# Windowed attention and a Mish layer: GpSimd keeps only the sums and maxima over partitions, and VectorE joins and splits the weights

## The chip, the cores and the metric

The kernel runs on one core of one Trainium2 chip. A core has five engines, each with its own queue of instructions that it works through in order, and they wait for each other through semaphores. TensorE (PE in the profile) multiplies matrices; the loading of its stationary operand is listed apart as PEld. VectorE is DVE, ScalarE is ACT, GpSimd is POOL, and SyncE (SP) only issues transfers here. ScalarE issues transfers too: all loads of the weights. The metric is the time of one execution on the device in microseconds (us).

## The reference

The program is an attention stage followed by a two-matrix layer. There are 8 batches of 8 heads; each head has 512 local positions and 32 global ones of width 64. A local query sees the 32 global keys and the local keys at a distance of at most 32. A global query sees everything.

```python
s_g = scale * np.matmul(q_g, k_all.transpose(0, 1, 3, 2))
out_g = np.matmul(sm(s_g), v_all)
s_ll = np.where(mask, s_ll, -1000000000.0)      # |i - j| <= 32
a_l = sm(np.concatenate([s_lg, s_ll], axis=-1))
out_l = np.matmul(a_l, np.concatenate([v_g, v_l], axis=2))
...
h = x @ w_in                                    # 4352 tokens, 512 -> 2048
g = h * np.tanh(np.log1p(np.exp(h)))            # for h <= 20
return (g @ w_out).astype(np.float32)           # 2048 -> 512
```

The inputs of the attention stage are 32-bit floats. The two weight matrices `w_in` and `w_out` arrive as 64-bit floats, and the kernel itself turns them into 32-bit ones from their two 32-bit words.

## The kernel before, in words

**Precision.** Matrix products run in 16-bit halves: an operand is scaled by a power of two, its high part is rounded to 16 bits, and its low part is what the rounding left. A product is then three matmuls (high by high, high by low, low by high). For the power of two, the kernel needs a maximum over all partitions (for the values `v`, one per batch) or a sum of squares over them (for each weight matrix). GpSimd makes both with `partition_all_reduce`: L504 for the maxima, L428 for the sums.

**The weights.** They come in 32 pieces of 512 KB, 16 for each matrix, loaded by ScalarE's queue (`w_load`, L379 and L383). For each piece, `w_bits` and `w_sum` build the 32-bit word. VectorE takes mantissa and exponent bits from the high word (L396), ScalarE turns the low word into a rounded integer `wr` (L398), VectorE puts in sign and top of the exponent (L405), and GpSimd adds `wr` as an integer (L407), so that a carry is right. Then TensorE adds the piece's squares into `ws` (`w_stat`, L417). After 16 pieces VectorE takes the diagonal of `ws` (L424), GpSimd sums it (L428), and a short chain gives the scale (L429 to L434). `w_split` then makes the halves, eight slots of 128x1024 for each matrix. For the first five slots of the first matrix, ScalarE or VectorE makes the high part directly and VectorE the low part (L452). For the other eleven, two ScalarE or VectorE steps make a scaled copy and the high part, and GpSimd subtracts them for the low part (L457).

**The attention.** 128 units (batch, pair of heads, 128 queries) run in a software pipeline: scores on TensorE (L613 for the first five head pairs in plain 32 bits, L620 after), a row minimum on VectorE (L626), exponentials on ScalarE (L635), high and low part of the result (L319, L654), a transposing transfer (L479), and the product with `v` (L671). Before any of it can be finished for the first batch, `v` has to be split with the scale that L504 to L512 make: L524 and L526 for the global rows, L319 and L573 for the local ones.

**The layer.** 17 blocks of 256 tokens in eight steps each: matmuls of the first matrix (`m1_mm`, L800), the Mish function on ScalarE (L843), high and low part (L321, L856), matmuls of the second matrix (`m2_mm`, L868). The first step of the first block stands at attention unit 17, and one step goes with each unit from there.

**What sets the order.** The program doesn't issue instructions as it meets them. `Plan.add` records each piece of work with an engine (or a choice of two), a cost in nanoseconds and what it reads and writes; `Plan.order` is a list scheduler that assigns start times from these costs, and the instructions are issued to the engines in that order. Weights have due times of their own (`CONV1`, `RATE1`, `FIRST1` and so on). A cost changed in `add` thus moves other instructions, on all engines. On the chip each engine keeps to its list, whatever the real durations are.

Of the kernel before, what the change touches and what calls it, by code (L numbers as in the profile page):

```python
# [226 lines left out]
def attn_mish_kernel(ctx: ExitStack, tc: tile.TileContext, qt, kt, qt0, kt0, vm, vg, qg, w1, w2, consts_in, out, w64):  # L227
# [13 lines left out]
    iww = const.tile([128, 1], F32, name="iww")  # L241
    W = const.tile([128, 18, 1024], F32, name="W")
# [5 lines left out]
    def rings(pool, *table):  # L248
        for tag, bufs, shape, dt in table:
# [5 lines left out]
          ("wr", 2, [128, 512], I32),  # L255
# [36 lines left out]
    def act(cols, acc=0):  # L292
        return 94 + 0.832 * cols + acc * 93
# [98 lines left out]
    def w_bits(k):  # L392
        if not w64:
# [4 lines left out]
        pl.add(ACT, act(512), lambda: A.activation(out=X["wr", k], in_=words(k).bitcast(U32)[:, :, 0], func=AF.Copy,  # L398
                                                   scale=2.0 ** -29), r=[rawkey(k)], new=[("wr", ("wr", k))])

    def w_sum(k):
        if not w64:
            return
        f, key = lambda: wf(k).bitcast(I32), wkey(*HV[k])
        pl.add(DVE, 680, lambda: V.scalar_tensor_tensor(f(), words(k)[:, :, 1], -0x40000000, f(), ALU.bitwise_and, ALU.bitwise_or),  # L405
               r=[rawkey(k)], w=[key])
        pl.add(POOL, 1400, lambda: G.tensor_tensor(f(), f(), X["wr", k], ALU.add), r=[("wr", k)], w=[key])  # L407
# [13 lines left out]
    def w_norm(w):  # L421
# [6 lines left out]
        pl.add(POOL, 4500, lambda: G.partition_all_reduce(X[p], X[m], 128, RED.add), r=[m], new=[("p2", p)])  # L428
# [11 lines left out]
    ON_POOL = 3  # L440

    parted = set()

    def w_split(j):
# [5 lines left out]
        if j < 8 - ON_POOL:  # L450
            pl.add([(ACT, act(1024)), (DVE, dve2(1024))], 0, lambda e: scaled(e, wh(j, 0), f, c), r=[k, ["sw", w]], w=[wslot(j)])
            pl.add(DVE, dve(1024), lambda: V.scalar_tensor_tensor(wh(j, 1), f, c, wh(j, 0), ALU.mult, ALU.subtract),  # L452
                   r=[k, ["sw", w], hi], w=[lo])
        else:
            pl.add([(ACT, act(1024)), (DVE, dve2(1024))], 0, lambda e: scaled(e, f, f, c), r=[["sw", w]], w=[k])
            pl.add([(ACT, act(1024)), (DVE, dve2(1024))], 0, lambda e: copy(e, wh(j, 0), f), r=[k], w=[wslot(j)])
            pl.add(POOL, 2230, lambda: G.tensor_tensor(wh(j, 1), f, wh(j, 0), ALU.subtract), r=[k, hi], w=[lo])  # L457

# [42 lines left out]
    def b_scale(b):  # L501

        m, p, sv = ("vmx", b), ("p2", b), ("sv", b)
        pl.add(POOL, 4500, lambda: G.partition_all_reduce(X[p], X[m][:, 5:6], 128, RED.max), r=[m], new=[("p2", p)])  # L504
# [565 lines left out]
    V.memset(pmax, 0.0)  # L1070
    for x in ORDER.split():
# [90 lines left out]
```

## Time and profile before

| what | value |
|---|---|
| median of 3 runs | 1037.8 us (1035.43 to 1037.85) |
| profiled execution, span | 1037.7 us, 20569 instructions |
| PE busy | 926.5 us (89%) |
| DVE busy | 664.3 us (64%) |
| ACT busy | 686.4 us (66%) |
| POOL busy | 85.2 us (8%), 62 instructions |

The profiled execution's time is its span, 1037.7 us, which is 0.1 us from the median of the runs. A page of the profile lists busy time by engine, the span in 40 slices of about 26 us with the busy share of each engine in tenths, and groups of instructions by line. A group's row names the line, the engine, the operation, output and input, a count, and then busy us, the mean ns of one, and the idle time of the engine just before, with the instruction that ended it. A row of the timeline is: start in us, duration in us, engine, line, operation, output<-input, and in square brackets the idle time just before and what ended it. "issue" there means that nothing which the profile records was waited for. GpSimd's loading of code is such a thing: it has no row as work.

### The profile page before, as it was taken

Reading aid. Unit: us, or ns where it says so; the run is one execution under the profiler, and the core shown is the slowest. Engines: PE = TensorE matmul, PEld = TensorE weight load, DVE = VectorE, ACT = ScalarE, POOL = GpSimd, SP = SyncE. Lnnn points to the kernel's source line nnn. Section 1 sums busy time; section 2 is a strip of 40 time slices with the busy share of each in tenths; the row PEclk is TensorE's granted clock in tenths of the full one; section 3 lists DMA queues with packets and bytes.
Section 4 is the critical chain, followed back from the end, with each engine's and each line's share of the span. In section 5 each row is a group of like instructions: output and inputs, shape, how many; then the busy total and the mean of one; then the engine's idle time right before and its main releaser. Section 6 shows DMA issues by size and latency. Waiting matters only on the chain.

```text
span 1037.7 us, 20569 instructions
## 1 busy us (share of the span) xinstructions
PE 926.5 (89%) x7906; PEld 665.6 (64%) x7906; DVE 664.3 (64%) x1697; ACT 686.4 (66%) x1327; POOL 85.2 (8%) x62
## 2 busy tenths in 40 slices
PE   3166558899999999999999999999999999999996
PEld 1044336567777777777777777677777777666663
DVE  4397977778766776677667766776676765422221
ACT  1257648677687888878887888788978887311110
POOL 3333531500000000000000000000000000000000
PEclk9997558999999999999999999999999999999998
DMA  9686792377866666667666665656675634100000
GB/s 358 232 199 138 158 197 83 88 162 161 187 145 140 145 144 151 136 144 143 138 150 143 136 140 136 148 121 140 145 157 120 141 75 79 28 21 21 1 21 21
DMA packets 231802, 134.65 MB, mean 130 GB/s; under 512 B 197528, under 2 KB 209048, under 8 KB 230680
## 3 DMA queue, kind: packets, MB, share of 16 engines
q1 hardware_dynamic: 225048, 116.56, 51.2%
q10 hardware_dynamic: 6656, 16.78, 5.0%
q8 instruction: 62, 1.02, 0.4%
q14 instruction: 36, 0.29, 0.1%
HBM read 63.55 MB, written 8.91 MB: 70 GB/s over the span
## 4 chain that ended last, share of the span: by engine, by line
PE 61%; DVE 11%; DMA 8%; ACT 6%; SPq 2%; issue 2%; POOL 0%; ACTq 0%; DVEq 0%; POOLq 0%
PE o L868 26%; PE h L800 25%; PE s L620 4%; DMA vraw<-in_vm 3%; PE U L671 3%; PE g L709 2%; DMA gpt<-gph 2%; SPq L308 2%; ACT L843 1%; PE gu L757 1%; DVE ph L654 1%; DVE P L626 1%; DVE vmx L493 1%; DMA W<-in_w 1%; ACT e L843 1%
## 5 line engine op out<-in xcount | busy, mean ns | idle before, releaser
L800 PE MATMUL h<-xh,W 128*128 128x256 f16 x2048 | 380.5, 275 | 11.0 <-ACT e L843 11.0
L868 PE MATMUL o<-W,G 128*128 128x512 f16 x1632 | 388.3, 379 | 0.2 <-POOL W L457 0.2
L800 PEld LDWEIGHTS <-W 128*128 128x128 f16 x3264 | 310.9, 98 | 74.2 <-issue 12.0
L800 PE MATMUL h<-xl,W 128*128 128x256 f16 x1024 | 281.3, 275 | 0.0
L868 PEld LDWEIGHTS <-G 128*128 128x128 f16 x1632 | 157.5, 98 | 145.9 <-issue 0.5
L843 ACT ACTIVATE e<-h,c 128x512 f32<-128x512 f32 (+1 forms) x137 | 92.8, 683 | 125.2 <-PE h L800 124.4
L626 DVE CUSTOM_DVE_ANT_0 P<-s,consts 128x192 f32<-128x192 f32 (+1 forms) x256 | 90.4, 366 | 86.8 <-PE s L620 84.5
L635 ACT ACTIVATE P<-P,nm 128x192 f32<-128x192 f32 (+1 forms) x256 | 118.0, 461 | 34.8 <-DVE nm L626 29.9
L321 DVE TENSOR_SCALAR G<-e,c 128x512 f16<-128x512 f32 x129 | 62.0, 480 | 120.2 <-ACT e L843 119.9
L654 DVE SCALAR_TENSOR_TENSOR ph<-P,ph 128x384 f16<-128x384 f32 (+1 forms) x128 | 80.6, 633 | 65.4 <-ACT ph L319 65.1
L856 DVE SCALAR_TENSOR_TENSOR G<-e,c,G 128x512 f16<-128x512 f32 (+1 forms) x137 | 103.8, 758 | 4.2 <-ACT G L319 1.0
L843 ACT ACT_TABLE_LOAD x78 | 100.1, 1283 | 1.4
L635 ACT ACT_TABLE_LOAD x75 | 96.2, 1283 | 1.3
L671 PEld LDWEIGHTS <-pt 96*128 96x128 f16 (+1 forms) x1536 | 59.3, 101 | 28.0 <-DMA pt<-ph 20.4
L319 ACT ACTIVATE ph<-P 128x384 f16<-128x384 f32 (+1 forms) x128 | 69.3, 546 | 12.1 <-DMA pt<-ph 9.1
L671 PE MATMUL U<-va,pt 128*128 128x64 f16 (+1 forms) x768 | 59.5, 200 | 16.4 <-DMA pt<-ph 15.1
L620 PE MATMUL s<-ks,qs 128*128 128x192 f32 (+1 forms) x216 | 70.7, 351 | 1.2 <-ACT gP L730 1.1
L417 PE MATMUL ws<-W 128*128 128x128 bf16 x128 | 18.9, 299 | 57.4 <-POOL W L407 57.2
L671 PE MATMUL U<-vc,pt 96*128 96x64 f16 x768 | 58.9, 198 | 0.0
L407 POOL TENSOR_TENSOR W<-W,wr 128x512 int32<-128x512 int32 x32 | 48.3, 1520 | 80.6 <-DVE W L405 17.7
L417 PEld LDWEIGHTS <-W 128*128 128x128 bf16 x128 | 10.9, 127 | 67.5 <-POOL W L407 65.1
L620 PE MATMUL s<-kl,qs 128*128 128x192 f32 (+1 forms) x216 | 54.2, 274 | 0.0
(102 smaller groups left out, 1049.8 us busy)
## 6 DMA issues: line engine op xcount, KB each, us to landing
kraw<-in_kt SPq DMA_DIRECT2D x27, 640.0 KB, 4.9
qraw<-in_qt SPq DMA_DIRECT2D x27, 512.0 KB, 3.8
W<-in_w ACTq DMA_DIRECT2D x19, 512.0 KB, 4.9
out<-ob SPq DMA_DIRECT2D x34, 256.0 KB, 2.6
vraw<-in_vm SPq DMA_DIRECT2D x8, 1024.0 KB, 5.9
wraw<-in_w ACTq DMA_DIRECT2D x13, 512.0 KB, 9.3
vc<-vf SPq DMA_DIRECT2D x32, 128.0 KB, 2.3
va<-vf SPq DMA_DIRECT2D x32, 96.0 KB, 2.3
```

The source lines that it names most:

```text
L319: A.activation(out=dst, in_=src, func=AF.Copy, scale=c)
L321: V.tensor_scalar(dst, src, c, None, ALU.mult)
L407: pl.add(POOL, 1400, lambda: G.tensor_tensor(f(), f(), X["wr", k], ALU.add), r=[("wr", k)], w=[key])
L620: T.matmul(X[s][:, :w], X[qs][:, h, t * 128:(t + 1) * 128], X[k][:, h, c0:c0 + w], start=(i == 0), stop=(i == 1))
L626: pl.add(DVE, 69 + 1.04 * w, lambda: V.tensor_tensor_reduce(out=X[P][:, h, :w], in0=X[s][:, :w], in1=mask[:, m0:m0 + w], scale=-SCALE, sca ...
L635: pl.add(ACT, 160 + 0.832 * w + 93, lambda: A.activation(out=X[P][:, h, :w], in_=X[P][:, h, :w], func=AF.Exp, bias=X[nm], scale=-1.0, accu ...
L654: pl.add(DVE, dve(n), lambda: V.scalar_tensor_tensor(p_part(X[ph], t, 1), p_src(X[P], t), PSC, p_part(X[ph], t, 0), ALU.mult, ALU.subtract ...
L671: T.matmul(X[u][:, t, h, :], X[pt][:k, p * 4 + h * 2 + c, :], X[vx][:k, t, vl, h * 64:(h + 1) * 64], start=(n == 0), stop=(n == 5))
L800: T.matmul(X[h][:, f * TB:(f + 1) * TB], wh(i, wl)[:, off:off + 128], X[x][:, d, o:o + TB], start=(n == 0), stop=(n == 11))
L843: chain(blk, i, ACT, 571, lambda a, z: A.activation(out=X[e][:, a:z], in_=hv(blk, i)[:, a:z], func=AF.Mish, bias=0.0, scale=X[c][:, 0:1]), ...
L856: chain(blk, i, DVE, 602, lambda a, z: V.scalar_tensor_tensor(gp(1, blk, i)[:, a:z], X[e][:, a:z], X["c", blk][:, 2:3], gp(0, blk, i)[:, a ...
L868: T.matmul(X[o], gp(g, blk, i)[:, f, t * 128:(t + 1) * 128], wh(8 + i, wl)[:, f * 512:(f + 1) * 512], start=(i == 0 and n == 0), stop=(i = ...
```

## The change

GpSimd's integer additions (L407) and subtractions (L457) go. VectorE puts in the low word itself, shifted by 29 bits and without rounding, in one more pass for each piece; ScalarE's conversion (L398) and its buffer `wr` go with the addition. All sixteen slots are split in the short way, with VectorE making every low part. GpSimd's list begins, behind its five memsets, with a maximum over a vector of zeros whose result nobody reads. The planner's cost for the sums and maxima goes from 4500 to 900, that of the dummy is 14000.

```diff
-          ("wr", 2, [128, 512], I32),
...
     def w_bits(k):
...
-        pl.add(ACT, act(512), lambda: A.activation(out=X["wr", k], in_=words(k).bitcast(U32)[:, :, 0], func=AF.Copy,
-                                                   scale=2.0 ** -29), r=[rawkey(k)], new=[("wr", ("wr", k))])
...
     def w_sum(k):
...
-        pl.add(DVE, 680, lambda: V.scalar_tensor_tensor(f(), words(k)[:, :, 1], -0x40000000, f(), ALU.bitwise_and, ALU.bitwise_or),
+        pl.add(DVE, 610, lambda: V.scalar_tensor_tensor(f(), words(k)[:, :, 1], -0x40000000, f(), ALU.bitwise_and, ALU.bitwise_or),
                r=[rawkey(k)], w=[key])
-        pl.add(POOL, 1400, lambda: G.tensor_tensor(f(), f(), X["wr", k], ALU.add), r=[("wr", k)], w=[key])
+        pl.add(DVE, 610, lambda: V.scalar_tensor_tensor(f(), words(k)[:, :, 0], 29, f(), ALU.logical_shift_right, ALU.bitwise_or),
+               r=[rawkey(k)], w=[key])
...
-        pl.add(POOL, 4500, lambda: G.partition_all_reduce(X[p], X[m], 128, RED.add), r=[m], new=[("p2", p)])
+        pl.add(POOL, 900, lambda: G.partition_all_reduce(X[p], X[m], 128, RED.add), r=[m], new=[("p2", p)])
...
-    ON_POOL = 3
...
-        if j < 8 - ON_POOL:
-            pl.add([(ACT, act(1024)), (DVE, dve2(1024))], 0, lambda e: scaled(e, wh(j, 0), f, c), r=[k, ["sw", w]], w=[wslot(j)])
-            pl.add(DVE, dve(1024), lambda: V.scalar_tensor_tensor(wh(j, 1), f, c, wh(j, 0), ALU.mult, ALU.subtract),
-                   r=[k, ["sw", w], hi], w=[lo])
-        else:
-            pl.add([(ACT, act(1024)), (DVE, dve2(1024))], 0, lambda e: scaled(e, f, f, c), r=[["sw", w]], w=[k])
-            pl.add([(ACT, act(1024)), (DVE, dve2(1024))], 0, lambda e: copy(e, wh(j, 0), f), r=[k], w=[wslot(j)])
-            pl.add(POOL, 2230, lambda: G.tensor_tensor(wh(j, 1), f, wh(j, 0), ALU.subtract), r=[k, hi], w=[lo])
+        pl.add([(ACT, act(1024)), (DVE, dve2(1024))], 0, lambda e: scaled(e, wh(j, 0), f, c), r=[k, ["sw", w]], w=[wslot(j)])
+        pl.add(DVE, dve(1024), lambda: V.scalar_tensor_tensor(wh(j, 1), f, c, wh(j, 0), ALU.mult, ALU.subtract),
+               r=[k, ["sw", w], hi], w=[lo])
...
-        pl.add(POOL, 4500, lambda: G.partition_all_reduce(X[p], X[m][:, 5:6], 128, RED.max), r=[m], new=[("p2", p)])
+        pl.add(POOL, 900, lambda: G.partition_all_reduce(X[p], X[m][:, 5:6], 128, RED.max), r=[m], new=[("p2", p)])
...
     V.memset(pmax, 0.0)
+    pl.add(POOL, 14000, lambda: G.partition_all_reduce(warm, pmax, 128, RED.max))
```

Three places of the instruction order are shown here, before and after. A row gives the line in the kernel concerned (lines below the edits move up by 8 or 9), the operation, the output, and behind the arrow the inputs.

The first is GpSimd's list from its last memset on. A row "ISA" with no operands is the loading of a set of operations into the engine; `vmx` holds the maxima of `v`, `wm` the diagonal of `ws`. Before:

```order
L281 MEMSET gph_80 64x1280
L407 ISA
L407 TENSOR_TENSOR W<-W,wr_115 128x512
L407 TENSOR_TENSOR W<-W,wr_134 128x512
L407 TENSOR_TENSOR W<-W,wr_152 128x512
L504 ISA
L504 ISA p_0_197<-vmx_154 128x1
L407 ISA
L407 TENSOR_TENSOR W<-W,wr_170 128x512
```

After:

```order
L281 MEMSET gph_81 64x1280
L1062 ISA
L1062 ISA warm<-pmax 128x1
L495 ISA p_0_181<-vmx_141 128x1
L427 ISA wp_399<-wm_391 128x1
L427 ISA wp_1474<-wm_1469 128x1
L495 ISA p_1_1492<-vmx_1152 128x1
```

Before, additions and maxima take turns, and each turn has a loading row: eight in the whole list. After, there is one such row, ahead of the dummy, and the rest of the list is ten sums and maxima.

The second is ScalarE's list around the split of the first batch's global rows of `v` (`vgf`), the first thing there that needs the scale from the first maximum. `wraw` and `W` behind "DMA" are loads of weight pieces. Before:

```order
L383 DMA wraw_195<-in_w 128x1024
L398 ACTIVATE wr_204<-W 128x512
L635 ACTIVATE P_0_1_138,sums_0_163<-P_0_1_138,nm_0_1_0_139 128x224
L319 ACTIVATE ph_72<-P_0_0_120 128x4x96
L383 DMA wraw_209<-in_w 128x1024
L383 DMA wraw_212<-in_w 128x1024
L398 ACTIVATE wr_225<-W 128x512
L524 ACTIVATE vgf_232<-vgraw_100,sv_217 128x128
```

After:

```order
L626 ACTIVATE P_0_0_117,sums_0_139<-P_0_0_117,nm_0_0_0_118 128x192
L379 DMA W<-in_w 128x2x512
L379 DMA wraw_150<-in_w 128x2x512
L379 DMA wraw_152<-in_w 128x2x512
L379 DMA wraw_158<-in_w 128x2x512
L383 DMA wraw_164<-in_w 128x1024
L383 DMA wraw_168<-in_w 128x1024
L383 DMA wraw_170<-in_w 128x1024
L515 ACTIVATE vgf_192<-vgraw_102,sv_184 128x128
```

In both, `vgf` stands behind the load of the nineteenth piece. The conversions `wr`, which waited for GpSimd's additions to free their two buffers, are gone from between.

The third is VectorE's list at the same place, from the first step on the maximum `p` on. Before:

```order
L508 TENSOR_SCALAR p_0_197<-p_0_197 128x1
L325 TENSOR_SCALAR p_0_197<-p_0_197 128x1
L328 TENSOR_SCALAR sv_217<-p_0_197 128x1
L329 RECIPROCAL sv_217<-sv_217 128x1
L511 TENSOR_SCALAR sv_217<-sv_217 128x1
L512 TENSOR_TENSOR pmax<-pmax,p_0_197 128x1
L396 TENSOR_SCALAR W<-W 128x512 x2
L526 SCALAR_TENSOR_TENSOR vgf_232<-vgraw_100,sv_217,vgf_232 128x128
L405 SCALAR_TENSOR_TENSOR W<-W 128x512 x2
L573 SCALAR_TENSOR_TENSOR vf_0_234<-vraw_96,sv_217,vf_0_234 128x4x128
```

After:

```order
L499 TENSOR_SCALAR p_0_181<-p_0_181 128x1
L325 TENSOR_SCALAR p_0_181<-p_0_181 128x1
L328 TENSOR_SCALAR sv_184<-p_0_181 128x1
L329 RECIPROCAL sv_184<-sv_184 128x1
L502 TENSOR_SCALAR sv_184<-sv_184 128x1
L503 TENSOR_TENSOR pmax<-pmax,p_0_181 128x1
L405 SCALAR_TENSOR_TENSOR W<-wraw_96,W 128x512
L517 SCALAR_TENSOR_TENSOR vgf_192<-vgraw_102,sv_184,vgf_192 128x128
L403 SCALAR_TENSOR_TENSOR W<-wraw_100,W 128x512
L396 TENSOR_SCALAR W<-W 128x512
L405 SCALAR_TENSOR_TENSOR W<-wraw_100,W 128x512
L403 SCALAR_TENSOR_TENSOR W<-W 128x512
```

The low part of `vgf` (L526 before, L517 after) stood behind the first passes on nine pieces of the weights; after, it stands behind those on four, so that more of the first matrix is behind it in VectorE's list. L403 and L405 of the changed kernel are the pass for sign and exponent and the new pass for the low word.

More of the change, by code (lines that the diff above doesn't have):

```diff
@@ L241, in attn_mish_kernel @@
     iww = const.tile([128, 1], F32, name="iww")
+    warm = const.tile([128, 1], F32, name="warm")
     W = const.tile([128, 18, 1024], F32, name="W")
```

## The prediction, on record before the result was known

> **What bounds the kernel now.** I read the slices of the span first, then busy time by stage, then the waits of TensorE, then the timelines of the engines that it waits for.
>
> ```profile
> PE   3166558899999999999999999999999999999996
> ```
>
> Each digit is the busy share in tenths of some 26 us. TensorE is full from the eighth slice on and far from it before.
>
> ```profile
> core 0: us, PE busy (x) PEld busy (x) DVE busy (x) ACT busy (x) POOL busy (x), PEclk, DMA share, GB/s
> 24.00:42.00 18.00, 0.23 (x3) 0.00 (x0) 2.77 (x11) 3.08 (x9) 1.53 (x2) 1.00 0.95 355
> 42.00:73.00 31.00, 19.50 (x110) 11.83 (x110) 28.90 (x60) 18.75 (x47) 17.68 (x14) 1.00 0.57 146
> 81.00:152.00 71.00, 42.89 (x323) 28.16 (x322) 62.25 (x139) 47.31 (x113) 28.95 (x16) 0.58 0.83 176
> 152.00:210.00 58.00, 50.69 (x387) 35.80 (x386) 43.60 (x90) 42.72 (x75) 21.71 (x12) 0.90 0.38 87
> 210.00:940.00 730.00, 715.82 (x6458) 526.35 (x6456) 489.96 (x1324) 555.63 (x1058) 4.95 (x6) 1.00 0.60 130
> ```
>
> From 210 to 940 us TensorE works 715.82 of 730 us, so no help to another engine shortens that. What can move is how long the stages before it take. From 24 to 42 us no compute engine does much. From 42 to 73 and from 81 to 152 us VectorE is nearly full (28.90 of 31, 62.25 of 71).
>
> ```profile
> PE ws L417 <- POOL W L407: 57.2, 19, 17.9
> 151.82 0.40 PE L800 MATMUL h<-xh,W 128*128 128x256 f16 x1
> ```
>
> The wait of TensorE that stands out is for GpSimd's additions: 57.2 us in 19 waits. The first matmul of the layer stands at 151.82, and 885.9 us follow it. I take that stretch as fixed but for its beginning (step 5) and ask when its first matmul comes.
>
> ```profile
> 4.27 1.16 POOL L281 MEMSET gph<- 64x1280 f16 x1
> 31.51 0.38 POOL L504 PARTITION_ALL_REDUCE p<-vmx  x1 [9.19 <-issue]
> 40.84 3.77 POOL L407 TENSOR_TENSOR W<-W,wr 128x512 int32<-128x512 int32 x3 [8.96 <-issue]
> 72.17 0.40 POOL L428 PARTITION_ALL_REDUCE wp<-wm  x1 [5.92 <-DVE gph L742]
> 79.52 2.49 POOL L407 TENSOR_TENSOR W<-W,wr 128x512 int32<-128x512 int32 x2 [6.95 <-issue]
> 166.30 0.40 POOL L428 PARTITION_ALL_REDUCE wp<-wm  x1 [6.48 <-issue]
> ```
>
> The first row is the last memset. The others are GpSimd's turns between additions and sums. A sum itself takes 0.4 us. Ahead of each turn the engine stands for 6 to 9 us with nothing recorded, and at each of these places the order has a loading row: this is code being fetched, 9 us where the transfers are dense and 6 to 7 later. (The 5.92 names a VectorE row that the sum does not read, so I count it as a fetch too.) By the Trainium skill, GPSIMD Engine Reference, section 2.1 Instruction dispatch, the first call after a load costs some 6 us that no row shows. By that figure these five would be 30 us instead of the 37.5 of the rows, and my sum 1 us smaller, in step 3.
>
> **The change, part by part.** Each step compares one point of VectorE's list with the same point before.
>
> *Step 1, the first maximum.*
>
> ```profile
> 14.93 0.15 DVE L499 TENSOR_REDUCE vmx<-vmx 128x1 f32<-128x5 f32 x1
> 30.81 0.33 ACTq L383 DMA_DIRECT2D wraw<-in_w  x1
> 31.92 0.15 DVE L508 TENSOR_SCALAR p<-p 128x1 f32<-128x1 f32 x1 [6.57 <-POOL p L504]
> 42.13 0.68 ACT L398 ACTIVATE wr<-W 128x512 int32<-128x512 uint32 x1 [11.55 <-POOL W L407]
> 43.13 0.35 DVE L526 SCALAR_TENSOR_TENSOR vgf<-vgraw,sv,vgf 128x128 f16<-128x128 f32 x1 [9.69 <-ACT vgf L524]
> ```
>
> The maximum's input is ready at 15.08; the result is used at 31.92. The fetch back to additions then holds GpSimd, this holds ScalarE's conversion until 42.13, that holds ScalarE's part of `vgf` behind it, and that holds VectorE until 43.13. After the change the code is fetched once, behind the memsets that end at 5.43. At the 9.2 us of a fetch among dense transfers it is there at 14.6, before the input, and the maximum follows at about 16. That cover is thin, but what comes next is later by far, so a fetch of 20 us would still cost nothing. ScalarE's part of `vgf` still stands behind the load of the nineteenth piece, issued at 30.81, and those issues keep pace with the transfers (share 0.95), not with GpSimd. So VectorE waits at its part of `vgf` from about 18 to 31.6 us, with most of the first matrix queued behind it in its list and TensorE's `ws` behind that. It restarts at 31.6 instead of 43.1. Issues 2 us sooner or later move that by as much.
>
> *Step 2, to the first sum of squares.*
>
> ```profile
> 67.87 0.07 DVE L424 DVE_READ_ACCUMULATOR2_ANT wm<- 128x1 f32 x1
> 72.60 0.15 DVE L429 TENSOR_SCALAR wp<-wp 128x1 f32<-128x1 f32 x1 [0.79 <-POOL wp L428]
> L396 DVE TENSOR_SCALAR W<-W x19: 374/419/1493, 16.7 to 156.9; 128x512 int32<-128x512 int32 x19
> L405 DVE SCALAR_TENSOR_TENSOR W<-W x19: 674/680/1760, 18.7 to 157.6; 128x512 int32<-128x512 int32 x19
> L405 DVE SCALAR_TENSOR_TENSOR W<-W 128x512 int32<-128x512 int32 x6 | 6.8, 1166 | 0.0
> L405 DVE SCALAR_TENSOR_TENSOR W<-wraw,W 128x512 int32<-128x512 int32 x5 | 4.2, 834 | 0.0
> L396 DVE TENSOR_SCALAR W<-W 128x512 int32<-128x512 int32 x4 | 4.8, 1220 | 0.0
> L396 DVE TENSOR_SCALAR W<-wraw 128x512 int32<-128x512 int32 x5 | 3.1, 629 | 0.0
> L626 DVE CUSTOM_DVE_ANT_0 P<-s,consts 128x224 f32<-128x224 f32 x7 | 2.6, 375 | 0.0
> ```
>
> The third and fourth rows give shortest, median and longest of one form in ns, the last five are groups from 43 to 81 us. One and the same shape takes 0.37 to 1.49 us on L396 and 0.67 to 1.76 on L405. GpSimd's additions run in just this stretch, and I read the excess as VectorE held off by them: 11.0 − 11 × 0.68 = 3.5 us on L405 and 7.9 − 9 × 0.42 = 4.1 on L396. The new pass has L405's shape and operands, so I price it at 0.68.
>
> From its restart to the sum's input VectorE's new list has 12 of L396 (5.0 us), 25 of the two other passes (17.0), 7 row minima at 0.37 (2.6), and smaller work: two low parts of `v`, 128x512 and so by 0.68; three low parts of exponentials, by 0.62 (a row of step 4); two maxima over 288 and 256 columns, an estimate of 0.4 each from L626's 0.37 for 224; and the 0.35 of `vgf`: 4.4 together. That is 29.0 us. With 1 us of waits (the old stage had 2.1 of 31) the input is ready at 61.6 instead of 67.9. Then the sum needs no fetch: 0.8 us, by 31.51 to 31.92 and a hop, instead of 4.7 to the row at 72.60. Its result is used at 62.4, a gain of 10.2 us.
>
> By the same prices the old list held 7 of L396, 9 of L405, 7 minima and the same smaller work between 43.1 and 67.6, 16.0 us of work in 24.5. Were that stretch of 1.53 VectorE's own, the new work would take 44.4 us: the bound on the other side.
>
> *Step 3, the way back.*
>
> ```profile
> 83.50 0.69 DVE L690 TENSOR_TENSOR xs<-x,xs 128x512 f16<-128x512 f32 x1 [6.33 <-ACT xs L312]
> ```
>
> While GpSimd fetches until 79.52, ScalarE stands at a conversion, and VectorE idles 6.33 us for the ScalarE work behind it. Afterwards there is neither fetch nor conversion: −6.3, in all −16.5.
>
> *Step 4, from there to the first matmul of the layer.*
>
> ```profile
> L405 DVE SCALAR_TENSOR_TENSOR W<-W 128x512 int32<-128x512 int32 x9 | 7.7, 862 | 0.0
> L452 DVE SCALAR_TENSOR_TENSOR W<-W,sw 128x1024 f16<-128x1024 f32 x5 | 7.3, 1459 | 0.0
> L654 DVE SCALAR_TENSOR_TENSOR ph<-P,ph 128x448 f16<-128x448 f32 x6 | 6.6, 1098 | 0.1
> L396 DVE TENSOR_SCALAR W<-W 128x512 int32<-128x512 int32 x9 | 5.2, 578 | 5.2 <-DMA W<-in_w 5.2
> L782 DVE TENSOR_TENSOR c<-sv,iw 128x1 f32<-128x1 f32 x2 | 3.3, 1650 | 0.0
> L550 DVE TENSOR_TENSOR qs<-qraw,qs 64x1024 fp32r<-64x1024 f32 x1 | 2.9, 2928 | 0.0
> L654 DVE SCALAR_TENSOR_TENSOR ph<-P,ph 128x448 f16<-128x448 f32 x53 | 32.5, 623 | 44.7 <-ACT ph L319 44.7
> L550 DVE TENSOR_TENSOR qs<-qraw,qs 64x1024 fp32r<-64x1024 f32 x24 | 29.3, 1222 | 0.7
> ```
>
> Six groups from 81 to 152 us, then two of the same lines from 210 to 940 us, where GpSimd is idle: 1098 against 623 ns, 2928 against 1222. The excess is 1.6 on L405, 1.4 on L396, 2.9 on L654, 3.0 on L782 (against 0.15, as for the 128x1 row L508), 1.7 on L550, and 1.2 on L452 (against 1.22, L550's for as many columns): 11.8 us. Added by the new order are 12 new passes (8.2) and three low parts of weights (3.7); one pass each of L396 and L405 goes (1.1), and the maxima over the next `v` come later now (four of 128x512 and two small ones, an estimate of 3.4 from the 0.68): 7.4 us. VectorE fills this stretch, so the difference counts: −4.4, in all −20.9, first matmul at 130.9. With no relief it is +7.4, with nothing added −11.8. What ScalarE loses I count as nothing, as it is busy 47.31 of 71 us here.
>
> *Step 5, behind the first matmul.*
>
> ```profile
> 171.67 6.92 PE h L800 x36
> ```
>
> This row of the chain follows the fetch before 166.30, behind which ScalarE and then TensorE are late. 36 matmuls take 6.92 us here, though the stage's other work leaves 7.3 us of 58 idle. Against that gain, eight low parts at 1.22 come to VectorE, which has 58 − 43.6 = 14.4 us free. I take −2, nearer to nothing than to the −7 that the idle time allows; the other end is +5, half of the added work.
>
> Sum: −10.2 − 6.3 − 4.4 − 2 = −22.9 on the span of 1037.7, which is 0.1 us from the median: **1015 us**. For this case by itself, 2 us of step 1 and half of the way to the ends of steps 4 and 5 make 1007 to 1023.
>
> **The rivals.** *Half the relief.* If GpSimd causes only half of the excess (8.5 us in step 2, 11.8 in step 4), 10 us are lost again: 1025. For it: transfers are dense in the same stages. Against it: 53 of L654 and 24 of L550 keep to 623 and 1222 ns with transfers at a share of 0.60.
>
> *VectorE becomes the bound (slower).* If the stretch is VectorE's own in this stage, the new passes stretch too. The sum's input is then ready at 31.6 + 44.4 = 76.0, 8.1 us late; 3.9 less for the sum and 6.3 for the way back leave −2.1; step 4 costs 7.4 × 62.25 / (62.25 − 11.8) = 9.1, step 5 its 5. That is +12, 1050 us. It decides from a mean of about 1.0 us on L405 on. By the Trainium skill, Perfetto Trace Analysis, section Optimizing Scalar/DVE Operations, a saturated VectorE speaks for moving work off it, even to GpSimd, though the page adds that the two share a port. The change does the reverse, and this rival is what that rule foretells.
>
> *More than counted.* If step 5 gives 7 us and step 4's wait of 5.2 for a weight piece goes as well: 1015 − 5 − 5.2 = 1005. For it: that piece's load is issued by ScalarE, which has less ahead of it.
>
> *The code does not stay loaded.* If each sum fetched again, 4 us of step 2 and step 5 would be lost: 1021. The order has one loading row; against it.
>
> *Nothing moves.* If the second matrix's late pieces hold the whole stage, the end stays at 1037. For it: the 5.2 us; against it: 57.2 us of other waits.
>
> **How the numbers follow.** My case 0.61, half the relief 0.14, more than counted 0.10, code not kept 0.03, nothing moves 0.05, VectorE the bound 0.07. A difference of 0.3% (3 us) is about what a measurement can tell from none. Faster is the first four, 0.88; same 0.05; slower 0.07. The range of 1001 to 1030 leaves out the last two and the far ends of the rest, some 0.17.
>
> **What would show it.** Right: one gap of 9 us on GpSimd, over by 15 us; `vgf` on VectorE near 31.6; the first sum's result used near 62; L396 and L405 at 0.42 and 0.68 without spread; no wait of VectorE like the 6.33; the first layer matmul near 131. Wrong: a spread that stays on these lines (the second and third case), a first matmul before 123 or after 139, or one in time with an end that does not follow, since then the stretch behind it is not fixed.

## The result, and the profile after

The changed kernel takes 1012.97 us (median of 4 runs, 1011.48 to 1017.32), the kernel before 1037.72 (4 runs, 1035.43 to 1037.85). The ratio is 0.9773, 95% interval 0.975 to 0.9796: 24.8 us faster by the medians, 23.5 by the ratio (0.0227 × 1037). The forecast was 1015. The profiled execution has a span of 1015.5 us and is the slowest of the four runs (1017.32 by its own time), so its end stands some 4 us above the median; the points inside it are compared with the same points of before. A run's time is some 1.8 us more than its span (1017.32 against 1015.5), so the profiled execution of the kernel before (span 1037.7) also stands above the median of its runs, by some 2 us and not by 0.1; below, spans are compared with spans and times with times.

First the slices of the span, and busy time by stage, after:

```profile
PE   2394598999999999999999999999999999999996
```

```profile
18.00:32.00 14.00, 1.67 (x10) 0.77 (x8) 1.16 (x3) 1.71 (x5) 0.00 (x0) 1.00 1.04 392
32.00:62.00 30.00, 19.81 (x102) 12.19 (x102) 29.93 (x88) 10.99 (x36) 0.39 (x1) 1.00 0.85 256
62.00:69.00 7.00, 6.50 (x57) 4.64 (x55) 7.00 (x21) 4.59 (x16) 0.00 (x0) 1.00 0.88 179
69.00:131.00 62.00, 35.05 (x276) 22.60 (x274) 51.36 (x128) 32.02 (x81) 0.00 (x0) 1.00 0.85 175
190.00:920.00 730.00, 715.71 (x6437) 525.46 (x6436) 489.00 (x1319) 551.20 (x1059) 4.30 (x6) 1.00 0.61 131
```

The columns of the stages are start and end, length, then busy us and instructions of PE, PEld, DVE, ACT and POOL, the granted clock, the share of the transfer engines and GB/s. TensorE is at eight tenths or more from the sixth slice on instead of the seventh, and at nine from the eighth instead of the ninth. The long stretch from 190 us on is what it was: 715.71 of 730 us. The gap with almost no compute is still there, from 18 to 32 us; behind it VectorE is full (29.93 of 30 us, 7.00 of 7).

Now the timelines of GpSimd and of VectorE after the change, by rows, and the first matmul of the layer:

```profile
5.57 0.38 POOL L1062 PARTITION_ALL_REDUCE warm<-pmax  x1
15.57 1.39 POOL L495 PARTITION_ALL_REDUCE p<-vmx  x1 [9.62 <-DVE vmx L490]
57.24 0.39 POOL L427 PARTITION_ALL_REDUCE wp<-wm  x1 [40.29 <-DVE wm L423]
157.45 0.55 POOL L427 PARTITION_ALL_REDUCE wp<-wm  x1 [99.83 <-DVE wm L423]
```

```profile
16.99 0.15 DVE L499 TENSOR_SCALAR p<-p 128x1 f32<-128x1 f32 x1 [0.24 <-POOL p L495]
31.27 0.35 DVE L517 SCALAR_TENSOR_TENSOR vgf<-vgraw,sv,vgf 128x128 f16<-128x128 f32 x1 [12.84 <-ACT vgf L515]
57.06 0.08 DVE L423 DVE_READ_ACCUMULATOR2_ANT wm<- 128x1 f32 x1
58.21 0.14 DVE L428 TENSOR_SCALAR wp<-wp 128x1 f32<-128x1 f32 x1
67.31 0.67 DVE L681 TENSOR_TENSOR xs<-x,xs 128x512 f16<-128x512 f32 x1
```

```profile
131.84 0.40 PE L791 MATMUL h<-xh,W 128*128 128x256 f16 x1
```

The first maximum and both sums on GpSimd now start 0.1 us behind their input, and the idle time ahead of each is put down to VectorE, none to "issue". VectorE's wait for its part of `vgf` ends at 31.27 (before 43.13), the first sum's result is used at 58.21 (72.60), the low half `xs` of the first attention output is made at 67.31 (83.50), and the layer begins at 131.84 (151.82). What follows its first matmul takes 1015.5 − 131.8 = 883.7 us (885.9). Of the 22.2 us between the two spans, 20.0 thus come before the layer's first matmul.

The forms of the three passes that make a weight's 32-bit word (shortest, median and longest in ns):

```profile
L396 DVE TENSOR_SCALAR W<-W x19: 395/419/428, 32.1 to 153.2; 128x512 int32<-128x512 int32 x19
L403 DVE SCALAR_TENSOR_TENSOR W<-W x19: 628/683/690, 33.1 to 154.2; 128x512 int32<-128x512 int32 x19
L405 DVE SCALAR_TENSOR_TENSOR W<-W x19: 669/681/690, 34.0 to 155.1; 128x512 int32<-128x512 int32 x19
```

The medians are those of before, and the long tail (1.49 and 1.76 us) is gone. The added pass (L405) costs what the old one (now L403) costs.

### The profile page after: what moved, and what is told of

The parts are those of the page before. It is cut to its first block, busy times and chain, and to the rows that moved or that the text cites. A ratio compares the mean times of both kernels' runs of the same rounds, so it can differ in the third digit from the quotient of the medians.

```text
span 1015.5 us, 20472 instructions
## 1 busy us (share of the span) xinstructions
PE 924.6 (91%) x7906; PEld 664.1 (65%) x7906; DVE 658.6 (65%) x1737; ACT 655.2 (65%) x1284; POOL 12.7 (1%) x20
## 4 chain that ended last, share of the span: by engine, by line
PE 62%; DVE 14%; DMA 13%; ACT 6%; issue 2%; SPq 2%; ACTq 0%
PE o L859 27%; PE h L791 25%; DMA gpt<-gph 4%; PE s L611 3%; DMA vraw<-in_vm 3%; PE U L662 3%; PE g L700 3%; DMA W<-in_w 2%; DMA pt<-ph 2%; PE gu L748 1%; SPq L308 1%; DVE P L617 1%; DMA ks<-in_kt 1%; ACT L834 1%; DVE W L403 1%
## 5 line engine op out<-in xcount | busy, mean ns | idle before, releaser
L321 DVE TENSOR_SCALAR G<-e,c 128x512 f16<-128x512 f32 (+1 forms) x131 | 62.8, 480 | 114.1 <-ACT e L834 113.7
L645 DVE SCALAR_TENSOR_TENSOR ph<-P,ph 128x384 f16<-128x384 f32 (+1 forms) x128 | 74.4, 582 | 68.3 <-ACT ph L319 68.0
L319 ACT ACTIVATE ph<-P 128x384 f16<-128x384 f32 (+1 forms) x128 | 69.8, 547 | 14.4 <-DMA pt<-ph 11.4
L721 ACT ACTIVATE gP<-g,gmx 64x288 f32<-64x288 f32 x64 | 30.4, 477 | 32.4 <-DVE gmx L716 30.9
L611 PEld LDWEIGHTS s<-ks,qs 128*128 128x128 f32 x216 | 41.2, 191 | 11.1 <-ACT gP L721 0.9
L626 ACT ACTIVATION_READ_ACCUMULATOR P<-P,nm 128x1 f32 x256 | 47.8, 187 | 0.0
```

The costliest lines, as they stand in the source:

```text
L319: A.activation(out=dst, in_=src, func=AF.Copy, scale=c)
L321: V.tensor_scalar(dst, src, c, None, ALU.mult)
L611: T.matmul(X[s][:, :w], X[qs][:, h, t * 128:(t + 1) * 128], X[k][:, h, c0:c0 + w], start=(i == 0), stop=(i == 1))
L626: pl.add(ACT, 160 + 0.832 * w + 93, lambda: A.activation(out=X[P][:, h, :w], in_=X[P][:, h, :w], func=AF.Exp, bias=X[nm], scale=-1.0, accu ...
L645: pl.add(DVE, dve(n), lambda: V.scalar_tensor_tensor(p_part(X[ph], t, 1), p_src(X[P], t), PSC, p_part(X[ph], t, 0), ALU.mult, ALU.subtract ...
```

## The experiments

The theory has two parts. One: every turn of GpSimd between additions and sums cost a fetch of code, and the waits behind it. Two: GpSimd's elementwise work stretched VectorE's passes. The rivals are that only one of them carries the gain, and that the layer's start was held by something else. The granted clock is one such thing: it reads 0.58 from 81 to 152 us before and 1.00 from 69 to 131 us after. That it is no part of the gain is shown in the last section.

### One half of the change at a time

The joins alone move to VectorE; the eleven low parts stay on GpSimd:

```diff
+    ON_POOL = 3
...
+        else:
...
+            pl.add(POOL, 2230, lambda: G.tensor_tensor(wh(j, 1), f, wh(j, 0), ALU.subtract), r=[k, hi], w=[lo])
```

> One part of the change alone: VectorE joins the low words, and GpSimd keeps the low parts of eleven slots, as in the kernel before. Theory: steps 1 to 3 of the prediction are kept, so the first sum's result is used near 58 us and the first layer matmul comes at 130 to 135; the second sum waits for a fetch of 6 us again, and the subtractions hold VectorE off in the stage behind it. 1016 to 1022 us. Rival (the low parts are the larger half of the gain): 1025 us or more.

Measured: 1015.94 us (1014.5 to 1019.33), ratio 0.9808 [0.9772, 0.9843]. The joins alone bring nearly all; what the low parts add, 0.9808 against 0.9773, is inside the intervals. GpSimd's rows of this run:

```profile
57.33 0.39 POOL L427 PARTITION_ALL_REDUCE wp<-wm  x1 [40.23 <-DVE wm L423]
103.84 2.64 POOL L456 TENSOR_TENSOR W<-W 128x1024 f16<-128x1024 f32 x1 [46.12 <-ACT W L312]
151.09 0.53 POOL L427 PARTITION_ALL_REDUCE wp<-wm  x1 [33.24 <-DVE wm L423]
```

The engine still changes between subtractions and sums, but the two changes shown fall into 46 and 33 us in which it has nothing else to do, and both sums start right behind their input: the fetch of 6 us that was expected ahead of the second does not show. (A third change, back to subtractions behind the second sum, falls into 7.43 us that the profile puts down to ScalarE.) In these runs a fetch costs time where work comes right before a sum; the additions were that work.

The other half: the low parts move, the joins stay on GpSimd, with the planner's old costs and no dummy.

```diff
...
-        pl.add(DVE, 610, lambda: V.scalar_tensor_tensor(f(), words(k)[:, :, 0], 29, f(), ALU.logical_shift_right, ALU.bitwise_or),
...
+        pl.add(POOL, 1400, lambda: G.tensor_tensor(f(), f(), X["wr", k], ALU.add), r=[("wr", k)], w=[key])
...
```

> The other part alone: VectorE makes all low parts, and GpSimd keeps adding the low words, with its fetches and without the dummy. Theory: steps 1 to 3 are gone, VectorE has three to eight more passes of 1.27 us, and only the fetch back behind the second sum is saved: 1030 to 1040 us, the first sum's result used at 70 to 75 us. Rival (the low parts are the larger half of the gain): 1020 to 1025 us.

Measured: 1045.24 us (1038.46 to 1046.72, 10 runs), ratio 1.0065 [1.0042, 1.0088]: slower than before, where 1030 to 1040 was expected.

```profile
70.86 0.40 POOL L430 PARTITION_ALL_REDUCE wp<-wm  x1 [6.10 <-DVE gph L736]
146.76 4.17 POOL L409 TENSOR_TENSOR W<-W,wr 128x512 int32<-128x512 int32 x3 [22.20 <-DVE W L407]
177.41 0.40 POOL L430 PARTITION_ALL_REDUCE wp<-wm  x1 [5.86 <-issue]
```

Both first reductions come about where they came before (30.46 instead of 31.51, 70.86 instead of 72.17), fetch included. The second matrix's sum comes at 177.41, 11 us later than the 166.30 of before: its joins stand idle up to 22.20 us for VectorE's passes, which now share VectorE with the low parts of the first matrix. That these low parts are what delays them was not tried by itself. The two halves do not add up (by the ratios 6.7 lost and 19.9 gained, against 23.5 for both): the low parts cost time while GpSimd's additions run, and none that shows once they are gone.

### Putting back each cost by itself

One column of pieces 15 and 31 is added to zeros on GpSimd, with an output that nobody reads, so that code must be fetched ahead of both sums, and nothing else changes.

```diff
...
+            if k % 16 == 15:
+                G.tensor_tensor(tout[:, :1], f()[:, :1], tin[:, :1], ALU.add)
...
```

> The changed kernel with two adds of one column on GpSimd, whose results nobody uses: one reads piece 15 of the weights when it is joined, one piece 31. Each makes GpSimd fetch the add's code and, behind it, the sum's code again ahead of the first and the second sum of squares. They take the port for next to nothing. Theory (a fetch ahead of a sum is paid in full where VectorE's list waits for the sum): GpSimd stands some 6 us ahead of each sum of squares, the first sum's result is used near 64 instead of 58.2 us, the first layer matmul comes 4 to 6 us later than 131.8, and the time is 1018 to 1022 us. Rival (other work hides the fetch): 1013 us, with the first layer matmul within 1 us of 131.8.

Measured: 1023.72 us (1022.44 to 1024.87), ratio 0.9876 [0.985, 0.9902]. By the ratios that is 0.0103 × 1037 = 10.7 us on top of the changed kernel (each ratio is known to some 0.0025, or 2.6 us); the time is 1.7 us above the range expected. GpSimd's rows, and the row of VectorE that uses the first sum:

```profile
55.78 0.85 POOL L410 TENSOR_TENSOR tout<-W,tin 128x1 int32<-128x1 int32 x1 [39.10 <-DVE W L408]
64.15 0.40 POOL L432 PARTITION_ALL_REDUCE wp<-wm  x1 [7.52 <-issue]
166.61 0.40 POOL L432 PARTITION_ALL_REDUCE wp<-wm  x1 [6.04 <-issue]
```

```profile
64.58 0.15 DVE L433 TENSOR_SCALAR wp<-wp 128x1 f32<-128x1 f32 x1 [6.32 <-POOL wp L432]
```

Behind an addition of a single column stand 7.52 us without work ahead of the first sum and 6.04 ahead of the second. VectorE uses the first result at 64.58 instead of 58.21, and the layer's first matmul comes at 136.9 instead of 131.8: 5.1 of the 6.4 us get through. Ahead of the second sum TensorE's wait for the first matmul of the second matrix (`o`, for ScalarE's high part) grows from 2.8 to 5.5 us. These two, 5.1 and 2.7, leave some 3 of the 10.7 us that no row here places, which is inside the uncertainty. By the Trainium skill, GPSIMD Engine Reference, section 2.1 Instruction dispatch, such a first call costs some 6 us that no row shows; the second of these agrees, the first, among dense transfers, is longer.

With 28 additions of a whole piece (128x512, for pieces 4 to 31), GpSimd's additions are put back in full (its subtractions are not), on top of the complete work of VectorE:

```diff
...
+            if k >= 4:
+                G.tensor_tensor(tout[:, :512], f()[:, :512], tin[:, :512], ALU.add)
...
```

> The changed kernel, with the 28 adds of 128x512 that GpSimd made for pieces 4 to 31 given back to it as dummies: each reads the joined piece and writes a scratch tile that nobody reads. The fetches ahead of the two sums come back as in the run with one-column adds, and GpSimd's adds run beside VectorE's passes as they did before. Theory (GpSimd's adds hold VectorE off): the means of the three passes over a piece go from 0.42 and 0.68 back to 0.6 to 0.8 and 0.9 to 1.1 us, VectorE's work from 31 us to the first sum stretches from 25.8 to some 33 to 36 us, the first layer matmul comes 15 to 25 us later, and the time is 1030 to 1040 us. Rival (the spread was VectorE's own or the transfers'): the passes stay at 0.42 and 0.68, and the time is that of the run with one-column adds, 1018 to 1022 us.

Measured: 1042.29 us (1037.25 to 1047.82, 10 runs), ratio 1.0052 [1.0027, 1.0077]. That is 0.0176 × 1037 = 18.2 us beyond the one-column additions, and 2 us above the range expected. The layer's first matmul comes at 152.68, 15.8 us later than with one column. In the same stretch of VectorE's list, from its part of `vgf` to the first sum's input, busy time by engine for the changed kernel, then for this one, with some of its groups:

```profile
31.20:57.20 26.00, 15.19 (x89) 9.24 (x90) 25.93 (x64) 7.41 (x21) 0.00 (x0) 1.00 0.85 270
```

```profile
31.20:67.00 35.80, 16.05 (x88) 9.27 (x89) 35.76 (x63) 7.38 (x21) 21.79 (x12) 1.00 0.63 199
```

```profile
L405 DVE SCALAR_TENSOR_TENSOR W<-W 128x512 int32<-128x512 int32 x9 | 8.6, 968 | 0.0
L408 DVE SCALAR_TENSOR_TENSOR W<-W 128x512 int32<-128x512 int32 x9 | 6.8, 768 | 0.0
L398 DVE TENSOR_SCALAR W<-W 128x512 int32<-128x512 int32 x9 | 6.6, 738 | 0.0
```

```profile
53.81 1.32 POOL L410 TENSOR_TENSOR tout<-W,tin 128x512 int32<-128x512 int32 x1 [1.77 <-DVE W L408]
53.93 0.38 DVE L622 CUSTOM_DVE_ANT_0 P<-s,consts 128x224 f32<-128x224 f32 x1
54.24 1.44 DVE L405 SCALAR_TENSOR_TENSOR W<-W 128x512 int32<-128x512 int32 x1
```

63 rows instead of 64, so the same work, take 35.76 us of VectorE instead of 25.93, while GpSimd works 21.79 us beside it. The groups are from that stretch (line, shapes, count, busy us, mean ns): 968 and 768 ns for passes of 683, 738 for one of 419. VectorE waits for no addition in that list. Transfers cannot be the reason, as they are less dense here (0.63 against 0.85).

Row by row the cause is plainer than in the means. Of the 12 additions in the stretch, each of the first eleven has exactly one VectorE instruction beside it that is lengthened, by 0.76 to 1.08 us; the eleven excesses add up to 9.9 us, which is the whole difference (35.76 − 25.93 = 9.8). All others keep their time. The last three rows show one such case: during an addition a row minimum keeps its 0.38 us, and the pass behind it takes 1.44 instead of 0.68. The row minima keep 0.34 to 0.38 us throughout, though six of the seven lie beside an addition, and the passes beside the first addition's row, which lasts 6.25 us, keep their 0.68 up to 40.09. So it is not GpSimd's being busy as such: an addition holds up one instruction of some kinds (the passes over a piece, low parts) and none of others (row minima). By the Trainium skill, Perfetto Trace Analysis, section Optimizing Scalar/DVE Operations, a saturated VectorE may be a reason to move work off it, even to GpSimd, but the two share a read port, so that this might not help. This run agrees with the caveat (18.2 us); that the port is what holds the passes is not shown by it.

So the two parts, put back singly, cost 10.7 and 18.2 us, together 28.9, where the change gained 23.5. This is no full account of the gain: both kernels keep the passes that the change added to VectorE, and neither puts back the turn around the first maximum (step 1), as VectorE's part of `vgf` stands at 31.24 in the last one. What step 1 is worth by itself was not tried; the kernel below with the loads on GpSimd has `vgf` 10.4 us earlier still and is some 6 us faster.

### The dummy maximum

```diff
-    pl.add(POOL, 14000, lambda: G.partition_all_reduce(warm, pmax, 128, RED.max))
+    pl.add(POOL, 14000, lambda: None)
```

> The changed kernel without the dummy's instruction, all other lists the same. The row that loads code stands at the same place of GpSimd's list, behind the memsets. Theory (the loading row starts the fetch by itself, and step 1 is held by ScalarE's loads until 31 us anyway): the first maximum's result is used within 1 us of 17 us and the time is 1013 us, within 0.3%. Rival (the fetch starts with the first call): the result is used at 23 to 26 us; as that is still ahead of 31 us, the time is 1013 us here too, and only GpSimd's rows tell.

Measured: 1014.76 us (two runs, 1014.64 and 1014.89), ratio 0.9776 [0.9746, 0.9805], no difference. GpSimd's row for the first maximum without the dummy:

```profile
15.50 1.39 POOL L495 PARTITION_ALL_REDUCE p<-vmx  x1 [10.07 <-DVE vmx L490]
```

It starts at 15.50 and takes 1.39 us, as it does behind the dummy (15.57, 1.39). The dummy is not what takes the fetch off the path. What does, as far as the rows show, is that nothing else stands on GpSimd's list between the memsets and the maximum.

### What is left ahead of the first sum

The longest wait in the new front is the 12.84 us of VectorE at `vgf`: ScalarE's part stands behind loads of weight pieces that ScalarE issues as transfers finish. The loads of pieces 4 to 18 go to SyncE's queue instead, at the same places in the program:

```diff
+            q = nc.sync if 4 <= k < 19 else nc.scalar
...
-                nc.scalar.dma_start(dst, w2[r0:r0 + 128, :])
+                q.dma_start(dst, w2[r0:r0 + 128, :])
...
```

> The changed kernel, with the loads of pieces 4 to 18 issued by SyncE instead of ScalarE, so that ScalarE's part of the global rows of v no longer stands behind the nineteenth load. Theory (VectorE's wait of 12.8 us at that part is on the path): VectorE goes on at 18 instead of 31.3 us, the first sum's input is ready at 44 to 48 instead of 57.1 us, the first layer matmul comes some 8 to 12 us earlier, near 121, and the time is 1001 to 1006 us. Rival (the transfers hold the stage): the pieces arrive no sooner, VectorE waits for them instead, the first sum's input comes at 52 us or later, and the time is 1009 to 1013 us.

Measured: 1008.89 us (1008.27 to 1011.89, 5 rounds), ratio 0.9729 [0.9706, 0.9752]: some 4.5 us better than the changed kernel by the ratios, though the intervals touch, and less than the theory's 1001 to 1006. Rows of VectorE, then one of ScalarE and one of SyncE:

```profile
18.46 0.34 DVE L518 SCALAR_TENSOR_TENSOR vgf<-vgraw,sv,vgf 128x128 f16<-128x128 f32 x1
53.02 0.62 DVE L646 SCALAR_TENSOR_TENSOR ph<-P,ph 128x448 f16<-128x448 f32 x1 [9.77 <-ACT ph L319]
55.46 0.08 DVE L424 DVE_READ_ACCUMULATOR2_ANT wm<- 128x1 f32 x1
```

```profile
52.41 0.58 ACT L319 ACTIVATE ph<-P 128x448 f16<-128x448 f32 x1 [13.90 <-DMA pt<-ph]
```

```profile
49.01 2.74 SPq L471 DMA_TRANSPOSE pt<-ph  x2
```

The wait at `vgf` is gone: 12.8 us earlier. But the first sum's input is ready only 1.6 us earlier, since VectorE now stands 9.77 us at a low part of exponentials, for ScalarE, which waits 13.90 us for a buffer that the first transposing transfer of `ph` has to read first. That transfer is issued at 49.01 (46.60 in the changed kernel), behind loads of weight pieces that now stand ahead of it in SyncE's queue (the last two of them issued at 40.38 and 40.85). The wait moved with the loads.

Two more kernels tell the queue from the transfers themselves. In one, the planner is told that these loads are SyncE's. In the other, the loads of pieces 10 to 18 go to GpSimd, which has nothing to do between its first maximum and the first sum; neither ScalarE nor SyncE then stands behind them. The edit of the second is this; that of the first has `nc.sync` and `DMA` for pieces 4 to 18 at the same places.

```diff
+            q = nc.gpsimd if 10 <= k < 19 else nc.scalar
...
-            pl.add(ACT, dma(512), go, ...
+            pl.add(POOL if 10 <= k < 19 else ACT, dma(512), go, ...
...
```

> As the kernel whose loads of pieces 4 to 18 are issued by SyncE, but with the planner told so, so that it places them on SyncE's list: the same 15 loads stand there together, and the second batch's queries and keys ahead of the last two. The theory that loads ahead of the first transpose on SyncE's queue hold it back says that it is issued at 46 to 50 us again, and the time 1006 to 1011 us; if it is the planner's ignorance of the queue that cost the time, it is issued before 45 us and the time is 1001 to 1006.

> The changed kernel, with the loads of weight pieces 10 to 18 issued by GpSimd, which is idle from its first maximum (17.0 us) to its first sum (57 us), instead of by ScalarE; the planner places them on GpSimd's list, behind the first maximum. Theory: with the loads on SyncE the low part of vgf came at 18.5 us instead of 31.3, but the first transpose of ph then stood behind loads on SyncE's queue and was issued at 49.0, and VectorE waited 9.8 us for it. Here neither ScalarE nor SyncE stands behind these loads, so vgf comes before 22 us, the first transpose of ph is issued before 45 us, the first sum's input is there before 53 us, and the time is 1001 to 1007 us. Rival: the transposes wait for the transfers themselves, whichever queue issues the loads (the DMA engines are full to 32 us): the first transpose is issued at 46 us or later and the time is 1007 to 1013. A second rival: issues on GpSimd are slow, or slow VectorE, so that pieces arrive late: over 1013.

Measured: SyncE, planned, 1012.36 us (1011.89 to 1014.45), ratio 0.9767 [0.9749, 0.9785]; GpSimd, 1007.5 us (1005.6 to 1009.71), ratio 0.9714 [0.9694, 0.9734]. For SyncE, planned, a row of SyncE's timeline; then for GpSimd a row of VectorE's timeline, one of SyncE's, and one of VectorE's waits:

```profile
48.00 2.74 SPq L471 DMA_TRANSPOSE pt<-ph  x2
```

```profile
53.44 0.08 DVE L424 DVE_READ_ACCUMULATOR2_ANT wm<- 128x1 f32 x1
```

```profile
43.98 5.40 SPq L471 DMA_TRANSPOSE pt<-ph  x2
```

```profile
DVE W L397 <- DMA W<-in_w: 6.5, 3, 3.9
```

A planner that knows the queue puts the same loads in the same place, and the transfer is still issued at 48.00, with VectorE waiting 8.9 us for the part behind it: the theory of the queue held for the transfer, and the total came out 1 us above what it gave. From the changed kernel this one can't be told (0.9767 against 0.9773), though its layer begins 4.2 us earlier, at 127.68; where those are lost again stays open. With the loads on GpSimd VectorE's part of `vgf` comes at 20.87 and the transfer is issued at 43.98, both as the theory expected. The sum's input comes at 53.44, 3.6 us earlier than in the changed kernel but 0.4 later than expected; VectorE's waits are now for the weight pieces themselves (6.5 us in three waits). The time of 1007.5 lies at the edge between the theory and the first rival. That rival's sign, a transfer issued at 46 us or later, did not come; the waits for pieces say that transfers have a share all the same. The kernel with the loads on GpSimd has the lowest median here. It beats the changed kernel by some 6 us, as the intervals lie apart (0.975 to 0.9796 against 0.9694 to 0.9734); from the one with SyncE (0.9706 to 0.9752) it can't be told.

## Why the prediction was right, and where it was not

| point of the list | before | predicted | measured |
|---|---|---|---|
| VectorE's part of `vgf` (step 1) | 43.13 | 31.6 | 31.27 |
| first sum's input (step 2) | 67.87 | 61.6 | 57.06 |
| its result used (step 2) | 72.60 | 62.4 | 58.21 |
| low half of the first output, `xs` (step 3) | 83.50 | 67.0 | 67.31 |
| first matmul of the layer (step 4) | 151.82 | 130.9 | 131.84 |
| from there to the end (step 5) | 885.9 | 883.9 | 883.7 |

The forecast was right in its sum and at four of six points. Between the first and the fourth of the table two errors cancel, 4.2 us too little gain in step 2 and 4.5 too much in step 3: that the fourth point came out within 0.3 us is luck.

**Step 1** held to 0.3 us, and for the reason given: ScalarE's part of `vgf` stands behind the nineteenth load in the changed kernel as well. That load is issued at 30.46 (30.81 before), and the part follows:

```profile
30.84 0.40 ACT L515 ACTIVATE vgf<-vgraw,sv 128x128 f16<-128x128 f32 x1 [6.32 <-DMA W<-in_w]
```

One detail of it, a gap of 9 us on GpSimd behind the memsets, does not show: the dummy's row begins at 5.57, and the stretch up to 15.57 is put down to VectorE's input. Whether code is fetched inside that stretch can't be seen.

**Step 2** was mis-sized by 4.2 us at the result (a gain of 14.4 instead of 10.2). The list of work was nearly right: the two passes over a piece together come 26 times where 25 were counted, L396 comes 12 times as counted, and the row minima, low parts and maxima as counted. The durations were right too. What failed is that they were added up. Rows of VectorE overlap:

```profile
33.08 0.69 DVE L403 SCALAR_TENSOR_TENSOR W<-W 128x512 int32<-128x512 int32 x1
33.69 0.42 DVE L396 TENSOR_SCALAR W<-W 128x512 int32<-128x512 int32 x1
34.02 0.68 DVE L405 SCALAR_TENSOR_TENSOR W<-W 128x512 int32<-128x512 int32 x1
34.62 0.68 DVE L403 SCALAR_TENSOR_TENSOR W<-W 128x512 int32<-128x512 int32 x1
```

A pass recorded with 0.68 or 0.69 us is followed by the next after 0.60 or 0.61, one of 0.42 after 0.33. A piece takes 1.54 us from start to start (33.08 to 34.62), where the durations add up to 1.79. Over the stretch, 61 rows whose durations add up to 30.7 us (the forecast had 29.0) took 25.8 us (31.27 to 57.06), and the 1 us of waits did not come.

**Step 3** gave 1.8 us instead of 6.3: from the sum's result to the low half `xs` it was 10.9 us and is 9.1. The wait of 6.33 for ScalarE is gone, as foretold. But the term took VectorE's other work there as unchanged, and the new list has more of it in that place: two passes of the added kind, three of L396 for one, seven row minima for three, and the two steps of `gph` (L321, L733), which VectorE did before while it waited for the sum. The row of the stage from 62 to 69 us above shows it: 7.00 of 7.00 us. The gain of a wait that ends is only what the work behind it leaves.

**Step 4** gave 3.8 us instead of 4.4 (64.5 us from there to the first matmul, before 68.3), and the inside of it was otherwise than put. Busy times in that stretch, before; then after, with a row of VectorE's timeline and one of the chain of waits:

```profile
83.50:151.82 68.32, 40.21 (x300) 26.07 (x300) 62.07 (x139) 44.63 (x106) 27.94 (x15) 0.56 0.86 182
```

```profile
67.30:131.84 64.54, 37.59 (x281) 24.12 (x282) 53.90 (x137) 34.52 (x91) 0.00 (x0) 1.00 0.85 176
```

```profile
91.56 0.75 DVE L564 SCALAR_TENSOR_TENSOR vf<-vraw,sv,vf 128x512 f16<-128x512 f32 x1 [6.86 <-ACT vf L319]
```

```profile
80.34 8.80 DMA gpt<-gph
```

VectorE's work fell by 8.2 us, more than the 4.4 that the relief less the added passes had made it; in part because L396 comes 10 times there instead of 13, where one less was counted. But a wait appeared that the step had not named: 6.86 us at a low part of `v`. ScalarE's part of it stands, in the chain of waits, behind a matmul for the global rows, and this behind a transposing transfer of 8.8 us. The wait for a weight piece shrank from 5.2 to 1.8 us. Together, −8.2 + 6.9 − 3.4 = −4.7, near the −3.8. So the −4.4 came near by another sum than the one given. The run with only the joins moved shows the same from the other side: GpSimd works 7.44 us in its stretch there and VectorE is busy 59.39 us, 5.5 more than here, and yet the layer's first matmul comes at 131.56. Since VectorE no longer sets the end of this stage alone, relief in it is worth little.

**Step 5** gave −2.2 us against −2, which is agreement in the number alone. The kernel without the dummy has 881.2 us behind its first matmul (span 1013.1, first matmul at 131.88) with otherwise the same program, so a figure of this size is not known better than to some 2 us. The row that the step starts from, 36 matmuls in 6.92 us, was misread as well: they start 0.19 us apart because they lie, but for the last microsecond, where the granted clock is 0.50 (170.7 to 177.5 us); at 1.00, from 156 to 166 us, matmuls of that form start 0.11 us apart. The changed kernel has such a stretch behind its second sum too (0.50 from 164.0 to 170.9 us), so that cost did not go with the fetch.

**The rivals.** Half the relief: refuted by the forms, which have no tail left. VectorE as the bound: its condition, a mean of about 1.0 us on the passes, is nearly met only where GpSimd adds (0.968 in the run with the full additions), and there the time is 1042. More than counted: step 5 gave 2.2 us instead of 7, and of the wait of 5.2 for a piece 3.4 went, but the new wait of 6.86 took more than that. Code that does not stay loaded: no sum has a gap. Nothing moves: refuted by the 23.5 us.

## What to carry to other kernels

Before giving elementwise work to an idle GpSimd, look at the spread of VectorE's rows of one shape while GpSimd works: here nothing but additions of no use beside it cost 18 us, and a single column ahead of each of two sums cost 11. Take single rows for it, not means: each addition lengthened one pass, and some kinds of instruction were never lengthened. Add up VectorE's work from start to start, not from recorded durations. When a wait is taken off a queue by moving transfers, look at what stands behind them in the queue that gets them; the queue of an idle engine gave the lowest median here, though not clearly ahead of SyncE's.

## What the runs showed that was not expected

A granted clock of 1.00 can stand for an empty record. In the kernel with the loads on SyncE the clock, third column from the end, reads 0.50 in a stage where the changed kernel has 1.00:

```profile
69.00:131.00 62.00, 37.56 (x277) 24.23 (x277) 54.20 (x139) 33.86 (x87) 0.00 (x0) 0.50 0.83 189
```

One form of TensorE (shortest, median and longest in ns) in that kernel from 32 to 131 us:

```profile
L663 PE MATMUL U<-va,pt x96: 232/242/255, 52.4 to 118.5; 128*128 128x64 f16 x72, 96*128 96x64 f16 x24
```

The same form in the changed kernel, from 32 to 131 us and from 190 to 920 us:

```profile
L662 PE MATMUL U<-va,pt x96: 232/242/258, 51.7 to 122.3; 128*128 128x64 f16 x72, 96*128 96x64 f16 x24
L662 PE MATMUL U<-va,pt x642: 190/193/207, 195.5 to 869.8; 128*128 128x64 f16 x135, 96*128 96x64 f16 x26
```

At readings of 0.50 and 1.00 the early matmuls agree to 3 ns, and the later ones, at 1.00, are 49 ns shorter. Their starts say it more clearly: back to back they start every 53 ns in both early stretches and every 29 ns from 190 us on. The trace of the changed kernel has no entry on the clock before 136.7 us, and the view then shows 1.00; the other's has 0.50 from 26.5 to 132.3 us. So TensorE went at about half its later pace in the early stages of both kernels. It did so in the kernel before as well, with 53 ns both from 43 to 73 us, where the clock reads 1.00, and from 90 to 145 us, where it reads some 0.5. The clock is thus no part of the gain: two runs of the changed kernel with mean readings of 0.939 and 0.996 took 1011.74 and 1011.48 us.

An issue of a weight load from GpSimd takes longer than one from SyncE (by their rows 0.55 to 0.90 us against 0.33 to 0.47), but VectorE's passes beside it keep their 0.68: it was elementwise work that stretched them, not GpSimd's being busy.
